# Decay rows issued by SyncE instead of ScalarE, weight loads spread out, and a new issue order, in a gated linear attention with a soft mixture of experts

## The chip, the cores and the metric

The kernel runs on one core of a Trainium2 chip. The metric is the device time of one execution in microseconds. A profile gives the span from the first to the last instruction of one execution and that execution's own time. Engines are named as in the profile: PE (matrix engine), DVE (vector engine), ACT (scalar engine), POOL (GpSimd), SP (SyncE, which here only issues DMAs). PEld is PE's weight load; ACTq and SPq are what the instruction sequencers of ACT and SP do themselves, such as issuing a DMA.

## The reference

Two stages follow each other. The first is a linear attention with a complex gate per step, for 4 batches, 8 heads, 768 steps and head dimension 48. The second treats the 3072 rows of 384 numbers that come out as tokens of a soft mixture of 8 experts with 4 slots each.

```python
scale = np.minimum(mag, 0.999) / (mag + 1e-06)          # mag = |a|
new_re = ar * S_re - ai * S_im
new_im = ar * S_im + ai * S_re
S_re, S_im = new_re + k v^T, new_im                      # per batch and head, for each t
y[:, :, t] = q^T S_re
...
logits = x @ phi                                         # x = y, 3072 x 384; phi 384 x 32
d = softmax of logits over the tokens;  slot_input = d.T @ x
slot_out[e] = relu(slot_input[e] @ w1[e]) @ w2[e]        # 384 -> 1024 -> 384
out = (softmax of logits over the slots) @ slot_out
```

## The kernel before, in words

**Blocks.** The time axis is cut into blocks of 128 steps: 24 blocks g (6 per batch), three of which make a unit u (8 units). Within a block the recurrence is written in polar form: sums of log magnitude and of phase over the steps come from a matmul with a triangular matrix, and queries and keys are scaled by exponentials of the magnitude and by sine and cosine of the phase. A state of 96x384 numbers carries from block to block within a batch.

**The stages and their names.** The whole front part is written as Python generators, one per piece of work, cut into steps at each `yield`. A string `ORDER` (L296) names, step by step, which generator runs next (`run`, L790); `_InOrder.pin` (L341) ties each engine to that order. A name that stands n times in the table runs n steps. Only the order within each engine counts; two neighbours in the table on different engines are free of each other. The names:

- `g` (gates, L603): for one unit, logarithms and exponentials of the gate, alternating DVE (L609, L615, L617, L621, L625) and ACT (L611, L613, L619, L623). The first unit is done in two parts (128x384 and 128x768), the others at once (128x1152). `t` is the arctangent (ACT L632). `L` and `T` load ACT's tables (L552 for exponential and logarithm, L555 for sine and arctangent).
- `p` (phase, L634): per block, a correction of one row from the block before (DVE L640), the matmul (PE L643, tile `up`), rounding (DVE L646, L648, tile `f`), sine and cosine (ACT L653, DVE L656, ACT L658, tile `cs`).
- `e` (expo, L663): per block the matmul (PE L667), two exponentials into the tile `ee` (ACT L671, L673), and then two small DMAs (L679) that copy the last step's row, 1x8x48, from `ee` to the tile `rrow`: the **decay rows**. There are 48 of them, and before the change ACT issues them.
- `d` (decay, L681): turns the three rows of a unit into columns `rt` (PE L684, DVE L686).
- `m` (mults, L690): multiplies `ee` in place by query and key (POOL L694; for block 0, DVE L699) and makes the tiles `hat` (DVE L703, twice a block). Because POOL overwrites `ee`, it must wait until the decay rows have been read out of it.
- `x` (transposes of `hat`, PE L715, copied by ACT L718 to `hT`), `c` (scores, PE L723, masked by DVE L727), `a` (output, PE L748 and L750, copied by ACT L753), `D` (state, PE L761, DVE L766 and L768), `f` (turns the output back, PE L773, ACT L776).
- `l`, `s` (router logits and running softmax sums), `me`, `er`, `si` (merging them, token weights, slot inputs).
- `la`, `lq`, `lv`: loads of the next unit's gates (1152 KB), queries and keys (1152 KB) and values (576 KB) into two buffers each, so that a load waits until the unit two before is done with its buffer. `w`: loads of expert weights: the first seven go to tiles of their own (`wx`, 1024 KB each), later ones into the buffers of `aat` and `qkt` and into freed memory. `wu` are matmuls without use. SP issues all of these loads in the order of the table.

After the table's end the experts run: hidden layer (PE L230), second layer (PE L250), mixing (PE L283), output DMAs (L289, L292). That part is the same code before and after.

Of the kernel before, what the change touches and what calls it, by code (L numbers as in the profile page):

```python
# [293 lines left out]


ORDER = """  # L296
    L0 lq0 w0 la0 w1 w2 w3 w4 w5 lv0 w6 g0 g0 wu1 g0 g0 wu2 g0 wu0 g0 wu3 g0 g1 g0 g0 g1 e0 g1 e0 g1 e0 e0 m0 T0 g1 t0 t1 p0 p0
    m0 p0 p0 p1 p0 L1 p1 m0 p1 x2 g1 x0 g1 p2 g1 p2 x0 g1 x2 p2 e1 g2 e2 la1 m0 g2 m0 g2 x1 x3 e1 g2 D0 e1 e1 D0 x1 x3 g2 c0 e2
    e2 c1 T1 c0 m1 c1 a0 e2 p1 a0 t2 p1 p1 p3 p2 p2 p3 m1 p2 L2 m1 x6 x4 p3 m2 x5 x4 x7 x6 d0 x5 d0 D0 x7 lq1 c2 p4 g2 c3 a0 g2
    p4 D1 c2 g2 D1 c3 a1 D1 g2 a1 D1 e3 m2 a1 e3 m2 x8 e3 x10 x8 p4 x9 x10 e3 x9 p5 e4 g3 e5 e4 e4 x11 m3 p5 x11 e4 D2 g3 p5 la2  # L300
    D2 g3 f0 D2 c4 m4 e5 e5 c5 c4 e5 T2 a2 c5 p3 p3 g3 a2 p3 p4 lv1 p4 d1 g3 f1 p4 a2 l0 p5 p5 m5 p5 l0 L3 d1 l0 l0 lq2 s0 s0 m3
    s0 g3 m3 f0 f1 g3 x13 x12 x14 s0 g3 x15 D3 x12 D3 g3 x14 x13 D2 x15 e6 m4 c6 e6 m4 e6 c7 e6 c6 x17 c7 x18 x17 D3 x16 m6 g4
    a3 x16 x18 a3 g4 D3 m5 e7 g4 x19 m5 e8 x19 g4 D4 a3 e7 D4 e7 e7 c8 g4 e8 e8 e8 c9 T3 c8 x22 c9 m7 t3 x21 D4 x20 x20 p6 x22
    m8 a4 x21 p6 a4 p6 p7 lq3 t4 p6 p7 D4 p6 x23 p7 c10 x23 c11 p8 p7 a4 p7 c10 p8 p7 c11 a5 la3 p8 a5 p9 m6 lv2 a5 m6 p8 x24
    x26 x24 p8 x25 m7 x26 x27 p8 l1 m7 L4 p9 l1 x25 D5 p9 x27 D5 g4 d2 c12 g4 c13 x29 d2 p10 g4 x28 p10 x28 g4 x29 c12 e9 p10
    x30 a6 x30 D5 e9 e10 p11 e9 c13 e9 e10 m8 e10 a6 e10 p11 m8 a6 e11 p11 m9 x31 la4 f2 x31 g5 D6 f2 D6 m10 g5 s0 f3 s0 g5 c14
    s0 f3 c15 c14 e11 e11 x32 c15 e11 T4 x33 D6 x34 D6 a7 x32 g5 x34 a7 p9 x33 p9 g5 p9 x35 D7 x35 m9 D7 t5 l1 m9 a7 p12 p10 p10
    l1 f4 m11 p10 f5 f4 p12 d3 f5 c16 d3 D7 p12 lq4 c17 p11 p11 c16 p11 x36 c17 L5 x37 p13 x38 a8 m10 s1 x36 s1 m10 s1 x38 a8
    x37 s1 D7 lv3 s1 a8 g5 p13 s1 l2 g5 x39 D8 x39 l2 s1 g5 D8 p13 c18 c19 c18 x40 c19 x42 x40 g5 x41 x42 x43 x41 x43 m11 e12
    e13 m11 e12 e12 a9 D8 e12 e13 D8 e13 a9 e13 p14 g6 p14 m12 a9 e14 p14 g6 D9 la5 D9 m13 g6 l2 l2 c20 s2 x44 s2 c20 c21 x44 D9  # L310
    e14 x46 c21 a10 x46 D9 e14 g6 T5 s2 a10 g6 e14 x45 x47 x45 s2 f6 x47 p12 f7 p12 m14 d4 f8 f6 d4 f7 c22 a10 t6 c23 c22 lq5
    p13 p13 a11 c23 p13 p15 f8 a11 m12 p14 p14 lv4 s2 m12 p14 x48 L6 s2 x50 s2 x49 m13 p15 x48 x50 x51 m13 x49 D10 x51 p15 D10
    a11 g6 l3 c24 g6 c25 l3 g6 c24 x54 x52 c25 x53 x52 g6 a12 x54 a12 D10 e15 a12 m14 x55 e15 e16 m14 e15 e15 x53 e17 p16 x55 g7
    D11 e16 e16 D11 e16 m15 p16 g7 D11 c26 g7 c27 c26 m16 e17 x58 e17 c27 x57 T6 a13 g7 e17 p15 a13 p15 g7 p15 x56 a13 l3 D12
    x56 l3 m17 x58 D12 t7 p16 x59 f9 p16 p16 lq6 d5 p16 d5 p17 f9 m15 x57 p17 x59 p18 m15 la6 f10 p18 f11 f10 f12 f11 p17 c28
    p18 f12 c29 p17 p17 c28 p17 x62 p19 L7 x61 c29 x60 D11 p19 s3 x63 x60 s3 D12 s3 x62 a14 s3 x61 D12 x63 m16 a14 m16 lv5 D13
    a14 p19 g7 D13 s3 g7 l4 c30 s3 g7 l4 s3 x64 c31 g7 x64 x66 c30 e18 x66 c31 x65 D13 e19 x65 m17 x67 a15 m17 x67 e18 D13 e18
    a15 e18 p20 p18 g8 p20 a15 e19 D14 e19 m18 p20 D14 e19 g8 e20 D14 g8 l4 l4 c32 w7 m19 c33 s4 e20 s4 c32 x69 e20 c33 T7 s4
    x68 s4 x70 g8 p18 a16 x69 x68 g8 a16 x70 e20 p19 x71 p19 m18 f13 p19 f14 x71 m18 c34 f13 f14 m20 a16 x72 c34 c35 x72 p20 x74
    p20 w8 s4 x74 p20 x73 s4 x75 L8 s4 d6 D15 d6 c35 x73 D15 D14 x75 a17 D15 g8 a17 g8 lv6 f15 m19 f16 g8 c36 m19 f15 c37 a17 g8  # L320
    f16 x77 x78 x77 c36 e21 c37 x76 a18 x76 m20 a18 x78 m20 D16 a18 e21 D16 e21 e21 e22 D16 e23 D16 e22 e22 x79 l5 x79 m21 e22
    e23 D17 l5 e23 T8 D17 l5 l5 f17 m22 e23 f18 t8 c38 f17 c39 f18 c38 m23 x80 c39 x82 x80 x81 x82 a19 x81 p21 a19 p21 a19 D17
    x83 p21 d7 x83 f19 c40 d7 p22 p21 f19 p21 c41 p21 c40 a20 c41 m21 a20 m21 x86 a20 D17 x85 x84 p22 x84 x87 x86 p22 l6 p22 p22
    D18 l6 p22 p23 D18 x85 m22 x87 p23 m22 l6 c42 w9 c43 c42 x90 c43 x88 l6 x89 x88 x91 x90 D18 a21 x89 p23 x91 a21 D18 p23 p23
    p23 D19 L9 m23 D19 c44 m23 w12 s5 x92 s6 s5 c44 s5 c45 a21 s5 x92 s6 D19 s6 s5 a22 s5 s6 s5 x94 c45 x93 x94 D19 a22 x93 x95
    c46 x95 a22 c47 c46 a23 c47 a23 f20 f21 f20 s6 a23 f21 l7 s6 f22 l7 s6 f23 f22 l7 l7 s7 me0 f23 w11 w10 er0 s7 me0 s7 er0
    er2 s7 er0 s7 er2 er7 er2 er1 er7 er7 s7 er8 ze0 er1 me0 er3 me0 s7 me0 er8 er6 me0 me0 er8 er6 me0 er3 er1 si0 er4 si0 er3
    er5 er6 er5 er4 er4 er5
"""


# [344 lines left out]
            rrow[u] = eo.tile([UB, H, 2, D], F32, name="rrow", bufs=1)  # L676
        r = LAST[par]
        for c in range(2):
            ACT.dma_start(out=rrow[u][j : j + 1, :, c, :], in_=e[r : r + 1, 0].rearrange("p (h d) -> p h d", d=D))  # L679
# [346 lines left out]
```

## Time and profile before

| what | value |
|---|---|
| three runs, median (lowest to highest) | 361.63 us (355.16 to 362.6) |
| the profiled execution | 356.5 us, span 354.7 us |
| mean granted PE clock | 0.906 of full |
| DMA moved | 54.85 MB, mean 155 GB/s |
| first stretch, 0 to 40 us | loads at 282 to 421 GB/s, PE short of work |
| middle, 40 to about 300 us | attention blocks, PE busy most of the time |
| end, from 308 us | experts and output |

A group line of the profile reads: source line, engine, operation, tiles (written <- read), count, then busy time, mean duration in ns, and the idle time of the engine just before these instructions with what ended most of it. A timeline line reads: start, duration, engine, line, operation, tiles, shapes, count, and in brackets the idle time before and what ended it. The chain that ended last is followed back from the last instruction: at each step to what released it. A line of the table by stretches has the stretch, its length, busy time of each engine with its count, the granted PE clock, the DMA engines' share, and GB/s.

### The profile page before, as it was taken

What the parts mean: (1) busy time and instruction counts of PE and PEld (TensorE: products, weight loads), DVE (VectorE), ACT (ScalarE), POOL (GpSimd) and SP (SyncE); (2) the same over time, 40 slices, a digit from 0 to 9 for tenths busy, and PEclk for the clock granted to TensorE, in tenths of its full rate; (3) what the DMA queues carried; (4) which work ended last, traced back from release to release, by engine and by line L of the source; (5) the groups of instructions that cost most, each with busy time, mean ns of one, the idle gap of its engine ahead of it and who ended that gap; (6) DMA issues with size and microseconds to landing.
All of it is one profiled execution on the core that took longest, in us unless ns stands there. A gap on an engine that the chain in (4) does not pass through costs nothing.

```text
span 354.7 us, 6884 instructions
## 1 busy us (share of the span) xinstructions
PE 301.5 (85%) x2758; PEld 229.2 (65%) x2758; DVE 244.9 (69%) x461; ACT 211.0 (59%) x373; POOL 46.6 (13%) x30
## 2 busy tenths in 40 slices
...
GB/s 264 421 420 419 246 81 71 258 9 1 135 188 13 136 111 23 69 20 140 178 2 1 266 71 1 122 118 68 3 0 2 120 354 409 145 284 421 200 290 105
DMA packets 15287, 54.85 MB, mean 155 GB/s; under 512 B 1936, under 2 KB 8976, under 8 KB 10640
## 3 DMA queue, kind: packets, MB, share of 16 engines
...
q10 hardware_dynamic: 768, 0.08, 0.2%
...
## 4 chain that ended last, share of the span: by engine, by line
PE 54%; DVE 20%; ACT 12%; issue 4%; DMA 4%; ACTq 3%; SPq 1%; DVEq 0%
PE sp L723 10%; PE tp L715 8%; PE up L643 5%; PE db L761 4%; PE hp L230 4%; PE yb L748 3%; PE op L250 3%; ACTq L679 3%; DVE scT L727 3%; DVE hat L703 3%; PE xp L773 3%; PE yb L750 3%; PE o L283 3%; PE lg L103 2%; DVE n L656 2%
## 5 line engine op out<-in xcount | busy, mean ns | idle before, releaser
L718 ACT COPY hT<-tp 96x512 f32<-96x512 f32 x96 | 51.7, 582 | 35.4 <-PE tp L715 31.9
L694 POOL TENSOR_TENSOR ee<-ee,qkt 128x768 f32<-128x768 f32 x23 | 43.8, 1905 | 216.0 <-DMA rrow<-ee 130.9
L715 PE MATMUL tp<-cst,hat 128*96 128x128 f32 x384 | 58.3, 298 | 11.2 <-DVE hat L703 7.6
L715 PEld LDWEIGHTS tp<-cst,hat 128*96 128x96 f32 x384 | 47.2, 138 | 24.6 <-issue 12.7
L723 PE MATMUL sp<-hT,hT 96*128 96x128 f32 x384 | 51.3, 287 | 1.8 <-ACT xs L776 1.0
L723 PEld LDWEIGHTS sp<-hT,hT 96*128 96x128 f32 x384 | 48.0, 201 | 3.5 <-ACT xs L776 1.2
L703 DVE TENSOR_TENSOR hat<-ee,cs 128x768 f32<-128x768 f32 x48 | 47.2, 1018 | 2.8 <-issue 1.4
L727 DVE TENSOR_TENSOR scT<-sp,cst 128x512 f32<-128x512 f32 x48 | 32.4, 686 | 15.3 <-PE sp L723 15.3
L643 PE MATMUL up<-aat,cst 128*128 128x384 f32 x48 | 24.8, 605 | 17.1 <-ACT aat L632 9.1
L748 PE MATMUL yb<-scT,vt 128*48 128x128 f32 x384 | 37.5, 282 | 1.3 <-DVE scT L727 1.0
L750 PE MATMUL yb<-hT,st 96*48 96x128 f32 x320 | 32.0, 278 | 0.0
L761 PEld LDWEIGHTS db<-vt,hat 128*96 128x96 f32 x320 | 29.7, 166 | 3.0 <-issue 1.9
L761 PE MATMUL db<-vt,hat 128*96 128x48 f32 x320 | 30.2, 248 | 0.0
L748 PEld LDWEIGHTS yb<-scT,vt 128*48 128x48 f32 x384 | 21.1, 124 | 8.2 <-issue 3.4
L643 PEld LDWEIGHTS up<-aat,cst 128*128 128x128 f32 x48 | 8.3, 215 | 22.6 <-ACT aat L632 10.2
L667 PE MATMUL lp<-aat,cst 128*128 128x384 f32 x48 | 21.4, 545 | 1.8 <-DVE aat L625 1.3
L646 DVE TENSOR_SCALAR n<-up 128x384 f32<-128x384 f32 x24 | 13.2, 550 | 13.9 <-PE up L643 13.9
L753 ACT COPY yT<-yb 128x512 f32<-128x512 f32 x24 | 14.0, 583 | 13.2 <-PE yb L750 10.9
L750 PEld LDWEIGHTS yb<-hT,st 96*48 96x48 f32 x320 | 19.7, 126 | 0.0
L658 ACT ACTIVATE cs<-n,kb 128x384 f32<-128x384 f32 x24 | 14.7, 611 | 6.7 <-DVE n L656 6.6
L623 ACT ACTIVATE gt<-aat,kb 128x1152 f32<-128x1152 f32 (+2 forms) x9 | 10.4, 1150 | 10.5 <-DVE aat L621 10.5
L671 ACT ACTIVATE ee<-lp 128x384 f32<-128x384 f32 x24 | 11.7, 488 | 7.7 <-issue 3.1
...
## 6 DMA issues: line engine op xcount, KB each, us to landing
qkt<-in_qk_dram SPq DMA_DIRECT2D x7, 1152.0 KB
aat<-in_aa_dram SPq DMA_DIRECT2D x7, 1152.0 KB
...
wx<-in_w_dram SPq DMA_DIRECT2D x5, 1152.0 KB
...
we<-in_w_dram SPq DMA_DIRECT2D x2, 1152.0 KB
wt<-in_w_dram SPq DMA_DIRECT2D x2, 1152.0 KB
```

The lines of the kernel that those rows point to most:

```text
L643: PE.matmul(out=up, lhsT=tri_u[par], rhs=ph, start=True, stop=True)
L658: ACT.activation(out=t[:, :, 0, :], in_=a.rearrange("p (h d) -> p h d", d=D), func=AF.Sin, scale=-TWO_PI, bias=kb[:, 2:3])
L667: PE.matmul(out=lp, lhsT=tri_l[par], rhs=aat[u][:, 0, j], start=True, stop=True)
L694: POOL.tensor_tensor(out=e, in0=e, in1=qkt[u][:, j], op=ALU.mult)
L703: DVE.tensor_tensor(out=x, in0=e[:, w].rearrange("p (h d) -> p h d", d=D).unsqueeze(2).broadcast_to([P, H, 2, D]), in1=cs[g], op=ALU.mult,)
L715: PE.transpose(out=tp[:, a, :], in_=hat[g][w][:, 4 * hh + a].rearrange("p c d -> p (c d)"), identity=ident)
L718: ACT.copy(out=hT[g, hh, w], in_=tp)
L723: PE.matmul(out=sp[:, a, :], lhsT=hT[g, hh, 1][:, a, :], rhs=hT[g, hh, 0][:, a, :], start=True, stop=True)
L727: DVE.tensor_tensor(out=t, in0=sp, in1=mask[g % 2].unsqueeze(1).broadcast_to([P, 4, P]), op=ALU.mult)
L748: PE.matmul(out=o, lhsT=vt[u][:, j, h, :], rhs=scT[g, hh][:, a, :], start=True, stop=first)
L750: PE.matmul(out=o, lhsT=st[g - 1][:, h, :], rhs=hT[g, hh, 0][:, a, :], start=False, stop=True)
L761: PE.matmul(out=db[:, h, :], lhsT=hat[g][1][:, h].rearrange("p c d -> p (c d)"), rhs=vt[u][:, j, h, :], start=True, stop=True)
```

## The change

Two edits. The decay rows are issued by SP instead of ACT:

```diff
         for c in range(2):
-            ACT.dma_start(out=rrow[u][j : j + 1, :, c, :], in_=e[r : r + 1, 0].rearrange("p (h d) -> p h d", d=D))
+            SP.dma_start(out=rrow[u][j : j + 1, :, c, :], in_=e[r : r + 1, 0].rearrange("p (h d) -> p h d", d=D))
```

And the table `ORDER` is another one with the same 1083 names. Its first line and its last ones show the kind of difference:

```diff
-    L0 lq0 w0 la0 w1 w2 w3 w4 w5 lv0 w6 g0 g0 wu1 g0 g0 wu2 g0 wu0 g0 wu3 g0 g1 g0 g0 g1 e0 g1 e0 g1 e0 e0 m0 T0 g1 t0 t1 p0 p0
+    g0 la0 wu1 L0 wu0 g0 g0 g0 g0 g0 g0 g0 wu3 g1 g1 g1 g1 e0 e0 e0 e0 T0 wu2 t0 p0 g1 g1 t1 p0 p0 p0 p0 lq0 L1 m0 m0 m0 x0 m0
...
-    s0 g3 m3 f0 f1 g3 x13 x12 x14 s0 g3 x15 D3 x12 D3 g3 x14 x13 D2 x15 e6 m4 c6 e6 m4 e6 c7 e6 c6 x17 c7 x18 x17 D3 x16 m6 g4
+    x14 x12 x12 x13 x13 x15 x15 p7 L3 g4 g4 g4 p7 m4 m4 m5 lv0 D3 c6 c6 D2 c7 x18 e6 e6 e6 e6 e7 e7 g4 x16 x16 e8 e7 e7 x17 x17
...
-    er5 er6 er5 er4 er4 er5
+    er5 er6 er5 er6 w10
```

The instructions are the same ones; each engine runs them in another order. Three places matter below.

**ACT at the start**, where the exponentials of block 0 end and the phase begins. Before:

```order
L671 ACTIVATE ee<-lp 128x384
L673 ACTIVATE ee<-lp 128x384
L679 DMA rrow<-ee 1x8x48 x2
L555 ACT_TABLE_LOAD
L632 ACTIVATE aat<-aat 128x384
L632 ACTIVATE aat<-aat 128x768
```

Now:

```order
L671 ACTIVATE ee<-lp 128x384
L673 ACTIVATE ee<-lp 128x384
L555 ACT_TABLE_LOAD
L632 ACTIVATE aat<-aat 128x384
L632 ACTIVATE aat<-aat 128x768
L653 ACTIVATE cs<-f 128x8x48
```

The two row DMAs are gone from ACT's queue, here and after each of the other 23 pairs of exponentials.

**SP**, after the ten loads of the first unit and the constants, which stay. Before:

```order
L567 DMA qkt<-in_qk_dram 128x2304
L596 DMA wx<-in_w_dram 128x2048
L563 DMA aat<-in_aa_dram 128x2304
L596 DMA wx<-in_w_dram 128x2048 x5
L571 DMA vt<-in_vv_dram 128x1152
L596 DMA wx<-in_w_dram 128x2048
L563 DMA aat<-in_aa_dram 128x2304
L567 DMA qkt<-in_qk_dram 128x2304
```

Now:

```order
L563 DMA aat<-in_aa_dram 128x2304
L679 DMA rrow<-ee 1x8x48 x2
L567 DMA qkt<-in_qk_dram 128x2304
L679 DMA rrow<-ee 1x8x48 x4
L563 DMA aat<-in_aa_dram 128x2304
L567 DMA qkt<-in_qk_dram 128x2304
L679 DMA rrow<-ee 1x8x48 x4
L596 DMA wx<-in_w_dram 128x2048
L679 DMA rrow<-ee 1x8x48 x2
L563 DMA aat<-in_aa_dram 128x2304
L571 DMA vt<-in_vv_dram 128x1152
L679 DMA rrow<-ee 1x8x48 x6
```

The rows stand between the loads and share SP's queue with them. Of the seven `wx` loads, one stands here, four more stand among the rows of units 3 to 6, and the last two stand behind the last row.

**DVE at the start**, from the rounded phase of block 0 on; `ee` and `hat_184` belong to block 0, 128x768 are the gates of the rest of unit 0, 128x1152 those of unit 1. Before:

```order
L703 TENSOR_TENSOR hat_184<-ee,cs 128x768
L646 TENSOR_SCALAR n<-up 128x384
L648 TENSOR_TENSOR f<-up,n 128x384
L621 SCALAR_TENSOR_TENSOR aat<-aat,gt 128x768
L640 SCALAR_TENSOR_TENSOR aat<-f,aat 1x384
L625 SCALAR_TENSOR_TENSOR aat<-aat,gt 128x768
L646 TENSOR_SCALAR n<-up 128x384
L648 TENSOR_TENSOR f<-up,n 128x384
L609 TENSOR_SCALAR gt,amin<-aat 128x1152
L699 TENSOR_TENSOR ee<-ee,qkt 128x384
L703 TENSOR_TENSOR hat_225<-ee,cs 128x768
```

Now, where the block's two `hat` tiles have the numbers 165 and 184:

```order
L703 TENSOR_TENSOR hat_165<-ee,cs 128x768
L699 TENSOR_TENSOR ee<-ee,qkt 128x384
L640 SCALAR_TENSOR_TENSOR aat<-f,aat 1x384
L621 SCALAR_TENSOR_TENSOR aat<-aat,gt 128x768
L703 TENSOR_TENSOR hat_184<-ee,cs 128x768
L625 SCALAR_TENSOR_TENSOR aat<-aat,gt 128x768
L609 TENSOR_SCALAR gt,amin<-aat 128x1152
L646 TENSOR_SCALAR n<-up 128x384
L648 TENSOR_TENSOR f<-up,n 128x384
```

The second `hat` of block 0 and the gates of unit 1 (L609) now stand ahead of the second block's phase, where they stood behind the third's.

More of the change, by code (lines that the diff above doesn't have):

```diff
@@ L305 @@
[L305 to L316, printed above, removed]
@@ L321 @@
[L321 to L324, printed above, removed]
@@ new lines @@
+    p1 p1 x2 g1 g1 g1 m0 x0 x3 x3 x1 g1 D0 g2 g2 e2 p1 p2 D0 g2 g2 g2 e2 e2 e2 m2 e1 e1 e1 e1 x1 x2 p2 g2 T1 p1 p1 c0 p2 c0 c1
+    d0 d0 D0 p1 a0 c1 t2 p2 a0 a0 p2 p2 la1 L2 m1 m1 x6 x6 m1 x4 D1 x4 g2 g2 D1 m2 f0 f0 x8 x8 x5 x5 p3 m2 p3 x7 x7 x9 x11 x11
+    g2 D1 e3 e3 e3 g3 p3 g3 D1 g3 c3 c3 c2 e4 x9 e4 e4 e5 e5 D2 c2 a1 g3 p4 lq1 e5 e5 x10 e4 m4 g3 g3 p4 w0 a1 a1 p4 p5 x10 g3
+    g3 c4 c4 p5 D2 p5 T2 c5 c5 a2 a2 t3 p6 p3 a2 g3 p3 D2 p3 p6 p5 p5 e3 m3 p4 p4 p5 f2 m3 m3 p7 p4 l0 l0 f2 la2 f1 f1 d1 d1 x14
@@ new lines @@
+    x14 x12 x12 x13 x13 x15 x15 p7 L3 g4 g4 g4 p7 m4 m4 m5 lv0 D3 c6 c6 D2 c7 x18 e6 e6 e6 e6 e7 e7 g4 x16 x16 e8 e7 e7 x17 x17
+    D3 x18 a3 c7 a3 g4 g4 a3 m5 x22 m5 x22 m6 p8 x19 e8 x19 e8 e8 g4 p8 D3 p8 g4 f3 g4 D3 x21 la3 f3 x20 c8 x21 c8 D4 T3 c9 c9
+    l0 D4 d2 t4 D4 x23 l0 p6 lq2 g5 a4 a4 d2 x20 c10 x23 c11 p7 p7 p6 p7 p9 p8 p9 a4 p6 D4 c10 p8 p8 a5 c11 a5 m6 x24 x26 p9 p10
+    m6 m7 L4 s0 a5 m7 m7 s0 s0 p10 p10 x27 x24 g5 g5 x27 x26 s0 lv1 D5 D5 D5 x25 x31 x31 m8 x25 x30 x30 x28 x28 e9 e9 e9 e9 c13
```

36 lines of the change are left out of this document (23 added, 13 removed).

## The prediction

> **What bounds the kernel now.** I read the page's busy times first, then the chain that ended last, then the stretches, then the timeline at the start and at one unit's border.
>
> ```profile
> PE 301.5 (85%) x2758; PEld 229.2 (65%) x2758; DVE 244.9 (69%) x461; ACT 211.0 (59%) x373; POOL 46.6 (13%) x30
> PE 54%; DVE 20%; ACT 12%; issue 4%; DMA 4%; ACTq 3%; SPq 1%; DVEq 0%
> by line: PE sp L723 9.7%; PE tp L715 8.1%; PE up L643 4.7%; PE db L761 4.4%; issue 4.0%; PE hp L230 3.5%; PE yb L748 3.4%; PE op L250 3.1%; ACTq L679 3.0%; DVE scT L727 2.9%; DVE hat L703 2.7%; PE xp L773 2.6%; PE yb L750 2.6%; PE o L283 2.
> L679 ACTq DMA_DIRECT2D rrow<-ee x48: 621/622/1232, 12.3 to 256.6; - x48
> ```
>
> PE is the busiest engine but holds only 54% of the chain; the chain jumps between engines, so each in-order queue matters. ACT computes for 211.0 us; the 48 row issues at 622 ns (median) add 48 x 0.622 = 29.9 us to its sequencer, and 3.0% of the 354.7 us span, 10.6 us, of them lie on the chain.
>
> ```profile
> 0.00:10.00 10.00, 4.63 (x8) 2.06 (x8) 3.65 (x11) 3.56 (x5) 0.20 (x4) 1.00 0.79 282
> 10.00:20.00 10.00, 3.08 (x6) 0.80 (x4) 4.70 (x11) 5.74 (x9) 0.00 (x0) 0.76 1.02 421
> 20.00:30.00 10.00, 7.80 (x16) 3.58 (x16) 8.33 (x13) 5.74 (x8) 0.00 (x0) 0.56 1.01 419
> 30.00:40.00 10.00, 6.55 (x58) 5.21 (x58) 6.92 (x10) 7.45 (x12) 2.29 (x2) 1.00 0.89 355
> 60.00:80.00 20.00, 15.16 (x145) 13.22 (x144) 15.93 (x27) 15.01 (x26) 3.94 (x2) 0.83 0.43 148
> 120.00:140.00 20.00, 17.73 (x144) 15.42 (x143) 14.53 (x28) 15.53 (x28) 4.68 (x3) 0.78 0.34 119
> 220.00:240.00 20.00, 16.43 (x128) 13.01 (x128) 13.02 (x23) 14.11 (x27) 5.46 (x3) 0.84 0.29 107
> 260.00:280.00 20.00, 19.74 (x223) 17.10 (x225) 14.26 (x29) 9.85 (x19) 0.20 (x1) 1.00 0.16 54
> 310.00:320.00 10.00, 10.00 (x84) 2.71 (x76) 0.42 (x1) 0.60 (x1) 0.00 (x0) 0.89 0.74 288
> ```
>
> Three regimes. To 40 us PE (first busy column) is short of work and the DMA engines are full. In the middle PE has 0.3 to 4.8 us idle in 20, and where it idles, the granted clock drops too (0.78 to 0.84). From 310 us PE is full and the code is unchanged.
>
> **The start.** ACT and PE up to the first sines, then where blocks 0 and 1 get their `hat`:
>
> ```profile
> 12.32 1.89 ACTq L679 DMA_DIRECT2D rrow<-ee  x2
> 14.24 1.28 ACT L555 ACT_TABLE_LOAD   x1 [1.57 <-issue]
> 15.53 1.26 ACT L632 ACTIVATE aat<-aat 128x384 f32<-128x384 f32 x2
> 16.11 1.65 PE L643 MATMUL up<-aat,cst 128*128 128x384 f32 x2 [4.51 <-ACT aat L632]
> 18.91 0.56 DVE L699 TENSOR_TENSOR ee<-ee,qkt 128x384 f32<-128x384 f32 x1
> 20.42 0.96 DVE L703 TENSOR_TENSOR hat<-ee,cs 128x768 f32<-128x768 f32 x1
> 27.34 1.34 DVE L609 TENSOR_SCALAR_CACHE_REDUCE gt<-aat 128x1152 f32<-128x1152 f32 x1
> 37.71 3.96 POOL L694 TENSOR_TENSOR ee<-ee,qkt 128x768 f32<-128x768 f32 x2 [37.25 <-ACT aat L632]
> 38.17 0.91 PE L643 MATMUL up<-aat,cst 128*128 128x384 f32 x2 [1.25 <-DVE aat L640]
> 39.93 3.42 DVE L703 TENSOR_TENSOR hat<-ee,cs 128x768 f32<-128x768 f32 x2
> 12.67 0.88 ACTq L679
> 13.58 5.20 DMA rrow<-ee
> 31.85 0.26 ACTq L679
> 32.15 0.62 ACTq L679
> 34.66 0.26 ACTq L679
> ```
>
> The last five rows are of the chain: a row issued at 13.58 landed 5.20 us later, while the loads ran at 421 GB/s. Now the table load follows the exponentials directly. The bracket is the gain: 1.57 us earlier for the table, the arctangent, `up` and the first sine. In the new DVE order unit 1's gates (27.34) stand ahead of the second phase instead of behind the third. By the rows above and the DVE work before them I put L609 about 2.2 to 3.5 us earlier: first `hat` at 20.42 - 1.6 = 18.8, ended 19.8; L640, L699 and L621 end near 21.8; second `hat` 1 us, L625 1 us, then L609 at 23.8 instead of 27.34. Against this, the second block's rounding comes behind L609, so its wrap and the third `up` are some 2 us later than before. The next common point is the `hat` of block 1, at 39.93, which followed POOL's first multiply (37.71 + about 2). POOL needs the rows of blocks 1 and 2; their exponentials follow unit 1's gates on ACT and come some 3 us earlier, and their rows land faster, since the seven weight loads no longer run then. Earliest case 6 us, latest 2 us (the two issues and nothing else). I take **-4.0 us**, nearer the middle, since both parts have a row.
>
> **The middle.** One unit's border:
>
> ```profile
> 86.62 1.28 ACTq L679 DMA_DIRECT2D rrow<-ee  x2
> 88.02 0.49 ACT L671 ACTIVATE ee<-lp 128x384 f32<-128x384 f32 x1 [1.06 <-PE sp L723]
> 88.54 1.27 ACTq L679 DMA_DIRECT2D rrow<-ee  x2
> 89.84 1.28 ACT L555 ACT_TABLE_LOAD   x1 [0.95 <-ACT ee L673]
> 91.14 1.16 ACT L632 ACTIVATE aat<-aat 128x1152 f32<-128x1152 f32 x1
> ```
>
> ACT's datapath stands idle 1.06 and 0.95 us while its sequencer issues rows, though the page names other releasers; behind it wait table, arctangent and the next `up`. So a pair of issues costs ACT about 1 us, not 1.25: the rest overlaps the exponential before it. Of the 10.6 us on the chain 2.0 (0.88 + 0.26 + 0.62 + 0.26) lie at the start, which is counted; 8.6 are left. If PE's own queue is next behind each (nothing won) the term is 0; if ACT alone was late, -8.6. PE with 54% and DVE with 20% of the chain are close behind, so I take half: **-4.3 us**.
>
> The clock: one minus the clock times 20 us is 3.4, 4.4 and 3.2 us of PE time lost in the three dipping stretches, 11.0 together. Shorter waits at the borders should save a little of it. Bounds: +3 (one more dip) to -8; I take **-2.0 us**, because the clock is low in the stretches where PE waits, and ACT's queue is one of several things it waits for there.
>
> **Rows on SP's queue.** The 29.9 us of issue move to SP, which computes nothing; its time is hidden as long as loads are not late. The cost is the row's way.
>
> ```profile
> 55.44 1.31 ACTq L679 DMA_DIRECT2D rrow<-ee  x2
> 57.97 1.81 POOL L694 TENSOR_TENSOR ee<-ee,qkt 128x768 f32<-128x768 f32 x1 [16.30 <-DMA rrow<-ee]
> 70.94 1.81 DVE L703 TENSOR_TENSOR hat<-ee,cs 128x768 f32<-128x768 f32 x2
> aat<-in_aa_dram SPq DMA_DIRECT2D x7, 1152.0 KB
> SPq L567 <- POOL ee L694: 73.1, 6, 25.8
> L703 DVE TENSOR_TENSOR hat<-ee,cs 128x768 f32<-128x768 f32 x48 | 47.2, 1018 | 2.8 <-issue 1.4 <-PE tp L715 1.0
> ```
>
> With quiet DMA engines a pair issued from 55.44 let POOL start at 57.97. POOL ends at 59.78, and the `hat` that reads it starts at 70.94: 11.2 us of slack; over the kernel DVE's `hat` waited 2.8 us, none of it mainly on POOL. A load of 1152 KB at 421 GB/s takes 2.8 us, so a row behind one is 2.8 us late, behind two 5.6. SP also holds a row while a load ahead waits for its buffer (73.1 us in six waits of L567). In the new order such a load waits for a multiply or a phase of an earlier unit, which POOL and PE run before that row's own multiply anyway. Each row also makes SP wait for ACT's exponential; queued behind it are the loads of a later unit, for which that unit's gates (DVE L609) and multiplies (POOL) wait, and their turn comes a unit later. I count **0**; bounds 0 and +19.6 (a load on each of seven units, nothing hidden).
>
> [...]
>
> **Weights.** Seven `wx` loads of 1024 KB leave the first 40 us; five run in the middle, where the DMA share is 0.16 to 0.43, two behind the last row. Covered by PE's work up to 310 us: 0. With that cover gone, two loads: 2 x 1024 KB at 421 GB/s, +5.0 us.
>
> **Sum.** 356.5 - 4.0 - 4.3 - 2.0 + 0 + 0 = 346.2, say **346 us**. The sum stands against the profiled execution (span 354.7, own time 356.5); the median of the three runs is 361.63, 1.4% above, so a median of the new kernel may lie as far above my figure.
>
> **Rivals.**
> 1. *PE hides it.* The issues on the chain are replaced by PE work of equal length, the clock does not move: 356.5 - 4.0 = 352.5. For: PE 19.74 of 20 us in 260 to 280. Against: 4.8, 2.3 and 3.6 us of idle in the three dipping stretches.
> 2. *Rows stuck behind loads.* The place is POOL's multiply ahead of `hat`, which DVE runs in order, so everything behind waits. It decides from the point where the new order leaves less time between a block's exponential and its `hat` than row, load and multiply take; then 2.8 us for each of seven units: 356.5 - 4.0 - 4.3 + 19.6 = 367.8. For: the 5.20 us row, SP's long waits. Against: 11.2 us of slack.
> 3. *The clock stays up.* PE's idle of 4.51 us before the first `up` shrinks to about 2.3 (1.57 earlier, and one spare matmul now between), and the clock, 0.76 and 0.56 from 10 to 30 us, stays full. `up` then takes 0.91 instead of 1.65 us; three of them make 2.2 us, and one whole dip of the middle saved makes 4.4: 346.2 - 2.2 - 4.4 = 339.6. [...]
>
> **How the numbers follow.** My sum 0.40, rival 1 0.27, rival 2 0.17, rival 3 0.16. Two per cent of 356.5 is 7.1 us, about what a measurement of this kernel can tell from no change: under 349.4 is faster, over 363.6 slower. The sum's own range, from the bounds of its terms, is 339 to 353; six sevenths of it is faster: 0.34, with rival 3 0.16 and a little of rival 1, 0.53. Slower: rival 2 and a bad order, 0.18. The rest, 0.29, is within. The range runs from 334, below rival 3, to 364, short of rival 2 in full.
>
> **What would show it.** Right: ACT's table load at about 12.7 us with no 1.57 us idle; block 1's `hat` near 36; no ACTq L679 on the chain; POOL's waits on rows still long but `hat` not waiting for POOL; the stretches 60:80, 120:140 and 220:240 at a higher clock. Wrong: DVE `hat` idle with POOL as releaser, rows landing over 5 us after issue in the middle (rival 2); PE's 4.8, 2.3 and 3.6 us of idle as before with no ACTq left on the chain (rival 1); hidden-layer matmuls waiting for weights.

## The result and the profile after

The changed kernel takes 318.06 us (median of four runs, 316.07 to 319.39), the kernel before 360.57 us in the same comparison (four runs). The ratio is 0.8896 with a 95% interval of 0.8761 to 0.9031: 11% faster, and 16 us below the lower end of the predicted range. Ratios here leave disturbed runs out, so they can differ by a per cent from the quotient of two medians.

The profiled execution took 316.07 us with a span of 314.2 us; before, 356.5 and 354.7. The busy times and the chain that ended last:

```profile
PE 280.0 (89%) x2758; PEld 220.8 (70%) x2758; DVE 242.4 (77%) x461; ACT 207.8 (66%) x373; POOL 54.1 (17%) x30
PE 53%; DVE 32%; ACT 7%; DMA 3%; issue 2%; SPq 0%; ACTq 0%; DVEq 0%
L703 DVE TENSOR_TENSOR hat<-ee,cs 128x768 f32<-128x768 f32 x48 | 47.5, 1018 | 0.6 <-ACT cs L658 0.4
```

PE runs the same 2758 instructions in 280.0 us instead of 301.5. So of the 40.5 us that the span lost, 21.5 are not fewer waits but a faster PE, and the other 19.0 are less idle time of PE (span minus busy: 53.2 before, 34.2 now). The mean granted clock says the same: one minus the clock times the span is 33.3 us of PE time lost before (0.906) and 11.9 us now (0.962). Of the 21.5 us, 19.1 lie between ACT's third load of the exponential table (40.7 us before, 35.3 now) and the first hidden-layer matmul (308.0 and 268.7), almost none before that, and 2.3 in the experts, whose code is the same. ACT's queue is gone from the chain, and `hat` waits for 0.6 us instead of 2.8.

The stretches that the prediction showed:

```profile
10.00:20.00 10.00, 4.68 (x12) 2.28 (x12) 6.19 (x11) 7.83 (x11) 0.00 (x0) 0.87 0.83 322
20.00:30.00 10.00, 9.24 (x50) 6.86 (x49) 8.91 (x14) 7.59 (x12) 0.63 (x1) 0.79 0.01 1
30.00:40.00 10.00, 8.08 (x61) 7.23 (x61) 9.65 (x13) 9.19 (x13) 2.96 (x2) 0.73 0.67 238
60.00:80.00 20.00, 18.45 (x172) 15.97 (x171) 19.84 (x28) 18.68 (x30) 8.90 (x4) 1.00 0.15 52
120.00:140.00 20.00, 20.00 (x198) 17.10 (x197) 17.50 (x30) 14.19 (x25) 7.78 (x4) 1.00 0.39 143
220.00:240.00 20.00, 19.92 (x233) 18.29 (x233) 13.07 (x26) 12.72 (x25) 1.49 (x1) 1.00 0.62 257
```

The three dips of the middle (0.83, 0.78, 0.84) are gone; the clock is full from 41 to 304 us. The DMA engines rest from 20 to 30 us, since the weights come later. At the start:

```profile
11.97 1.55 SPq L679 DMA_DIRECT2D rrow<-ee  x2
12.34 1.28 ACT L555 ACT_TABLE_LOAD   x1
14.21 0.91 PE L643 MATMUL up<-aat,cst 128*128 128x384 f32 x2 [1.93 <-ACT aat L632]
22.60 1.35 DVE L609 TENSOR_SCALAR_CACHE_REDUCE gt<-aat 128x1152 f32<-128x1152 f32 x1
29.37 3.59 POOL L694 TENSOR_TENSOR ee<-ee,qkt 128x768 f32<-128x768 f32 x2 [28.91 <-DMA rrow<-ee]
33.10 1.81 DVE L703 TENSOR_TENSOR hat<-ee,cs 128x768 f32<-128x768 f32 x2
```

The table load follows the exponentials with no bracket, `up` takes 0.91 instead of 1.65 us, and block 1's `hat` starts at 33.10 instead of 39.93.

### The profile page after: what moved, and what is told of

Same layout as the page of the kernel before. It is cut to its first block, busy times and chain, and to the rows that moved or that the text cites. A ratio compares the mean times of both kernels' runs of the same rounds, so it can differ in the third digit from the quotient of the medians.

```text
span 314.2 us, 6918 instructions
## 1 busy us (share of the span) xinstructions
PE 280.0 (89%) x2758; PEld 220.8 (70%) x2758; DVE 242.4 (77%) x461; ACT 207.8 (66%) x373; POOL 54.1 (17%) x30
## 4 chain that ended last, share of the span: by engine, by line
PE 53%; DVE 32%; ACT 7%; DMA 3%; issue 2%; SPq 0%; ACTq 0%; DVEq 0%
PE tp L715 9%; PE sp L723 7%; DVE hat L703 7%; PE db L761 5%; PE yb L748 4%; PE op L250 4%; PE hp L230 3%; DVE scT L727 3%; PE yb L750 3%; DVE aat L621 3%; PE up L643 3%; PE o L283 3%; PE xp L773 2%; DVE f L648 2%; DVE n L646 2%
## 5 line engine op out<-in xcount | busy, mean ns | idle before, releaser
L694 POOL TENSOR_TENSOR ee<-ee,qkt 128x768 f32<-128x768 f32 x23 | 51.4, 2246 | 169.6 <-DMA rrow<-ee 123.1
L715 PE MATMUL tp<-cst,hat 128*96 128x128 f32 x384 | 56.3, 285 | 8.8 <-DVE hat L703 8.7
L715 PEld LDWEIGHTS tp<-cst,hat 128*96 128x96 f32 x384 | 44.2, 132 | 18.1 <-issue 13.3
L761 PEld LDWEIGHTS db<-vt,hat 128*96 128x96 f32 x320 | 32.3, 173 | 2.3 <-issue 1.1
L761 PE MATMUL db<-vt,hat 128*96 128x48 f32 x320 | 32.6, 252 | 0.1
L748 PEld LDWEIGHTS yb<-scT,vt 128*48 128x48 f32 x384 | 21.1, 122 | 12.0 <-DVE scT L727 6.8
L643 PE MATMUL up<-aat,cst 128*128 128x384 f32 x48 | 21.6, 533 | 3.5 <-ACT aat L632 2.4
L667 PE MATMUL lp<-aat,cst 128*128 128x384 f32 x48 | 19.5, 498 | 0.0
L646 DVE TENSOR_SCALAR n<-up 128x384 f32<-128x384 f32 x24 | 13.2, 550 | 5.5 <-PE up L643 5.4
L776 ACT COPY xs<-xp 128x384 f32<-128x384 f32 x24 | 11.1, 476 | 8.5 <-PE xp L773 8.4
L285 ACT ACTIVATE os<-o,rc 128x256 f32<-128x256 f32 (+1 forms) x24 | 9.7, 420 | 9.7 <-PE o L283 7.1
L287 DVE TENSOR_SCALAR os<-o,rc 128x256 f32<-128x256 f32 (+1 forms) x24 | 9.8, 417 | 8.1 <-PE o L283 5.9
```

The source lines that it names most:

```text
L643: PE.matmul(out=up, lhsT=tri_u[par], rhs=ph, start=True, stop=True)
L646: DVE.tensor_scalar(out=n, in0=up, scalar1=MAGIC, scalar2=MAGIC, op0=ALU.add, op1=ALU.subtract)
L667: PE.matmul(out=lp, lhsT=tri_l[par], rhs=aat[u][:, 0, j], start=True, stop=True)
L694: POOL.tensor_tensor(out=e, in0=e, in1=qkt[u][:, j], op=ALU.mult)
L715: PE.transpose(out=tp[:, a, :], in_=hat[g][w][:, 4 * hh + a].rearrange("p c d -> p (c d)"), identity=ident)
L748: PE.matmul(out=o, lhsT=vt[u][:, j, h, :], rhs=scT[g, hh][:, a, :], start=True, stop=first)
```

## The experiments

Theory at this point: two of the change's parts are worth more than the prediction gave them, because each wait of PE that goes also spares a stretch at half clock, and the new order itself shortens the middle, which the sum had not counted. Rival: one part (the rows off ACT) does it all, and order and weights only ride along. The early or spread weights, which belong to the new table, are taken as a part of their own. All kernels compute the full result; some add useless work, which is said there. "Idle" is span minus PE busy, "clock" is span times one minus the mean granted clock, both of the profiled execution; half clock during a wait counts in both, so the two must not be added. Diffs of the table show pieces of its lines.

| run | order | rows issued by | weights | median us | ratio, 95% interval | span | idle | clock |
|---|---|---|---|---|---|---|---|---|
| before | old | ACT | early | 360.57 | 1 | 354.7 | 53.2 | 33.3 |
| D | old | ACT | spread | 349.88 | 0.987, 0.978 to 0.996 | 347.9 | 50.7 | 26.4 |
| E | old | SP | early | 360.43 | 1.021, 1.007 to 1.034 | 360.3 | 65.8 | 34.6 |
| C | old | SP | spread | 339.17 | 0.958, 0.948 to 0.967 | 336.3 | 44.4 | 22.5 |
| B | new | ACT, late | early | 343.46 | 0.970, 0.959 to 0.981 | 341.4 | 51.7 | 26.6 |
| A | new | ACT, late | spread | 347.45 | 0.978, 0.968 to 0.989 | 346.4 | 51.3 | 31.9 |
| G | new | ACT | spread | 331.26 | 0.941, 0.928 to 0.954 | 329.2 | 42.0 | 21.7 |
| F | new | SP | early | 338.73 | 0.961, 0.942 to 0.980 | 335.9 | 57.1 | 21.8 |
| the change | new | SP | spread | 318.06 | 0.890, 0.876 to 0.903 | 314.2 | 34.2 | 11.9 |

The kernel before had medians from 355.25 to 360.57 us in the six comparisons.

### The three parts, each alone and together (A to G)

A, B and G are the new order with the rows on ACT. In A and B they stand where the new table has them; in G directly behind the block's exponentials:

```diff
-            SP.dma_start(out=rrow[u][j : j + 1, :, c, :], in_=e[r : r + 1, 0].rearrange("p (h d) -> p h d", d=D))
+            ACT.dma_start(out=rrow[u][j : j + 1, :, c, :], in_=e[r : r + 1, 0].rearrange("p (h d) -> p h d", d=D))
```

B and F load the weights early again, and with them the first loads of unit 1 (the first line of the new table reads `g1 g1 g1 g0` ahead of its first `e0`, not four times `g1` as printed in the section on the change):

```diff
-    g0 la0 wu1 L0 wu0 g0 g0 g0 g0 g0 g0 g0 wu3 g1
+    lq0 w0 la0 w1 w2 w3 w4 w5 lv0 w6 g0 wu1 L0 wu0 g0 g0 g0 g0 g0 g0 g0 wu3 g1
```

C and D are the old order with the seven weight loads spread (C with the rows on SP too), E the old order with only the rows on SP:

```diff
-    L0 lq0 w0 la0 w1 w2 w3 w4 w5 lv0 w6 g0 g0 wu1
+    L0 lq0 la0 lv0 g0 g0 wu1
...
-    la2 D2 g3 f0 D2 c4
+    la2 w0 D2 g3 f0 D2 c4
```

The expectations:

> The new order and the spread weights, with the decay rows issued by ACT again. If the order of the stages brought the gain (theory ORDER), most of the 42 us stays: 318 to 328 us, PE clock still near 1.00 from 60 to 300 us. If the freed ACT queue brought it (theory ROWS), the time goes back by the 17 us of ACT idle or more, with its clock dips: 340 to 358 us. If the quiet DMA engines brought it (theory LOADS), nothing changes: 316 to 320 us.

> The new order of all compute stages, but rows on ACT and the seven weight loads at the start as before: only the order of the stages is new. ORDER: 320 to 332 us, the start a few us later than in the change. ROWS or LOADS: back near before, 345 to 360 us.

> The old order of the stages, with both DMA edits: rows on SP, weights spread. ORDER: the ACT queue's freed time gives what the prediction gave it, 4 to 10 us, so 347 to 356 us. ROWS: most of the gain, 318 to 335 us.

> The old order of the stages with rows on ACT; only the seven weight loads move from the start to places behind later units' loads. ORDER or ROWS: within 4 us of before (355 to 361 us), the rows of block 0 landing in about 2 us instead of 5. LOADS: 335 us or less.

> The new order and the spread weights, rows on ACT, but each pair of rows directly behind its two exponentials in ACT's queue, not at the late place that the new table gives SP. In the run with the rows at that late place PE stood idle 7.4 us for one row that ACT issued behind two gate operations. If that lateness was most of the 29 us between that run and the change (theory LATE ROWS), this gives 322 to 332 us. If the 48 issues themselves cost the time in a queue that the new order fills (theory ISSUE TIME), it stays at 338 to 350 us.

> The kernel before with the rows on SP and nothing else: the first rows now stand behind seven weight loads of 1024 KB in SP's queue. Rows stuck behind loads: block 0's first multiply (DVE L699) waits until some 30 us instead of 18.9, time 350 to 362 us, 10 us or more over the run with spread weights and rows on SP. If rows pass loads, 336 to 342 us as in that run.

> The change with the seven weight loads, and the first loads of unit 1, at the start as before. Rows stuck behind loads: the start is late by 10 to 15 us, time 328 to 335 us. If rows pass loads: 316 to 322 us.

What was measured, by the table. A lies in the range of ROWS, G in that of LATE ROWS, E in that of rows stuck behind loads; B, C and D lie between the ranges of their theories, and F 4 us above its higher one. No part brings the gain alone. From before to the change one part at a time: weights spread, about -5 us (D's ratio of 0.987; 7 by the medians, 357.15 to 349.88); rows to SP, -10.7 (D to C); new order, -21.1 (C to the change). Undone from the change's side, the rows are worth 13.2 us (G), the weights 20.7 us (F). So the parts are not independent. With rows on ACT the spread weights are worth some 5 us in the old order, and in the new one with its late rows they even cost 4 (B 343.46, A 347.45, with intervals that overlap). With rows on SP they are worth 21 us in either order (E to C 21.3, F to the change 20.7), because without the spreading the first rows stand behind the loads. The queue of SP and the chain in F:

```profile
9.55 5.10 SPq L596 DMA_DIRECT2D wx<-in_w_dram  x5
22.14 28.48 SPq L679 DMA_DIRECT2D rrow<-ee  x6
```

```profile
9.55 15.00 DMA wx<-in_w_dram
24.57 13.41 DMA rrow<-ee
38.10 0.57 DVE ee L699
```

SP, still issuing loads, reaches the first rows only at 22.14. The second of them, issued at 24.57, lands 13.41 us later, at 37.98, and the first DVE multiply of `ee` follows at once. PE waits 23.6 us there in one piece, 3.39 in the change. E has the same row (13.43 us) and a wait of PE of 23.2 us. That is rival 2 of the prediction, real and of its size, but at one place and hidden by the third part of the change. Before the change, on ACT's queue beside the same loads, this row landed 5.20 us after its issue (13.58).

A against G shows that the place of the issue in ACT's order matters as much as the issue. In A it stands behind the gates, and PE idles 7.39 us. A's chain there:

```profile
130.90 1.07 ACT aat L611
131.99 0.67 ACT gt L613
132.69 2.52 DMA rrow<-ee
135.37 1.81 POOL ee L694
137.21 0.97 DVE hat L703
138.22 1.09 PE tp L715 x4
```

So A and B price the new order too low; G (331.26) is the fair one, 18.6 us below D.

### Where in the kernel the order's 21 us lie (I, J, M to P)

The first guess was one mechanism: in the old table the arctangents of units 2, 4 and 7 come in the same period of ACT's sine table as the unit's first phase, right ahead of it; in the new table all come a period earlier. I moves two of them ahead in the old order (base C), J moves six back in the new one, each with the first phase steps behind it:

```diff
-    p4 a2 l0 p5 p5 m5 p5 l0 L3 d1 l0
+    p4 a2 l0 p5 p5 m5 p5 l0 t3 L3 d1 l0
```

```diff
-    p5 T2 c5 c5 a2 a2 t3 p6 p3 a2 g3 p3
+    p5 T2 c5 c5 a2 a2 p3 a2 g3 p3
...
-    T3 c9 c9 l0 D4 d2
+    T3 t3 p6 p6 p7 p7 p7 p8 p8 p8 c9 c9 l0 D4 d2
```

> The table of before with the rows on SP and the weights spread (339.17 us, ratio 0.9575), and in it the arctangents of units 2 and 7 moved one trigonometric period of ACT ahead, with the gate steps of their unit that they need. The order is then the old one in all else. Theory 'arctangent a period ahead' (the new table is faster because a unit's gates and arctangent are done a whole period before its first phase, so that PE does not stand before the first up): PE's waits of over 2 us before the up of these two units go, and the time is 4 to 8 us below 339, 331 to 335 us (ratio 0.934 to 0.946). Rival 'no single place' (the gain of the new table is spread over many small waits, the arctangent was not what PE waited for once the rows were off ACT): 337 to 341 us, and the gaps stay or come up elsewhere.

> The changed kernel, with the arctangents of units 2 to 7 moved one period of ACT later, behind the table load of the unit's own first phase, and the first phase steps that stood ahead of it moved behind them. Nothing else is changed. Theory 'arctangent a period ahead': PE stands before the first up of these units for 1.3 to 2.5 us each, as it did in the kernel before (2.34, 2.27 and 2.98 us at three places), and the clock drops behind some of them: 8 to 15 us above 318, 326 to 333 us (ratio 0.914 to 0.934). Rival 'no single place': 316 to 322 us (ratio 0.885 to 0.903), since up has other work of PE ahead of it.

I: 344.62 us, ratio 0.972 (0.964 to 0.981), 5 us slower than C. J: 384.82 us, ratio 1.086 (1.074 to 1.098), 67 us slower than the change, over four times the most that was expected. J's largest group of PE's waits (sum, count, longest) and one of its units:

```profile
PE up L643 <- DVE aat L640: 29.4, 13, 5.5
```

```profile
125.05 1.16 ACT L632 ACTIVATE aat<-aat 128x1152 f32<-128x1152 f32 x1
126.25 0.55 DVE L640 SCALAR_TENSOR_TENSOR aat<-f,aat 1x384 f32<-1x384 f32 x1 [2.81 <-ACT aat L632]
126.85 1.43 PE L643 MATMUL up<-aat,cst 128*128 128x384 f32 x2 [4.14 <-DVE aat L640]
130.10 1.65 PE L643 MATMUL up<-aat,cst 128*128 128x384 f32 x2 [1.82 <-DVE aat L640]
```

J lays the chain arctangent, `up`, rounding, row correction, next `up` bare three times a unit: about 3.3 us from one `up` to the next, on PE. It shows what a late arctangent costs when nothing stands between the three phases. It doesn't show that the old order pays this: there other work stands between them, and I won nothing, since with the rows off ACT (C) PE no longer waited at those two places. The guess falls.

The second approach splices the two orders (rows on SP, weights spread): one table up to an ACT table load, then what is left in the other order. The cuts are the third and the fifth load of the exponential table, at 35.3 and 87.5 us in the change.

```diff
     a0 c1 t2 p2 a0 a0 p2 p2 la1
-    L2 m1 m1 x6 x6 m1 x4 D1 x4
+    lv0 m1 p3 p3 m1 L2 m1 x6 x4 p3 x5 x4 x7 x6
```

(The change and M around the first cut; O has the same at the second, N and P the counterparts.)

> Rows on SP and weights spread, as in the change. The new table up to ACT's third load of the exponential table (35.3 us in the changed kernel, 41.7 in the kernel that has the old table), then what is left in the old order. Between the old table throughout (339.17 us, ratio 0.9575) and the change (318.06, 0.8896) lie 21 us. Theory 'start': they come from the first 80 us, where the change has 8.2 of its 10.2 us less idle of PE; this kernel wins at least the 6.4 us of the earlier load: 326 to 333 us (ratio 0.92 to 0.94). Theory 'later': they come from the order behind it, and the early lead is lost again at the next common wait: 336 to 340 us.

> The counterpart: the old table up to the same load, then what is left in the new order. Theory 'start': 324 to 332 us, as the 6.4 us of the start are missing. Theory 'later': 316 to 321 us (ratio 0.885 to 0.90). If this one and its counterpart together win much less or much more than 21 us, the parts depend on each other.

> As the first of these, with the cut at ACT's fifth load of the exponential table (87.5 us in the change, 101.2 with the old table). Theory 'start': nearly the whole gain is there, 318 to 324 us (ratio 0.89 to 0.91). Theory 'later': the gain comes in equal parts along the middle, so about a third of it is missing and the 13.7 us at the cut are what stays, 325 to 331 us (ratio 0.91 to 0.93), or less if it is lost again.

> The counterpart of the third: the old table up to ACT's fifth load of the exponential table, then the new one. Theory 'start': 334 to 339 us (ratio 0.94 to 0.957), nothing left to win. Theory 'later': 328 to 333 us, the 7 us behind the cut are won.

| run | median us | ratio, 95% interval |
|---|---|---|
| M: new to the first cut, then old | 338.40 | 0.952, 0.945 to 0.960 |
| O: new to the second cut, then old | 330.90 | 0.928, 0.918 to 0.938 |
| N: old to the first cut, then new | 326.86 | 0.912, 0.902 to 0.922 |
| P: old to the second cut, then new | 342.08 | 0.959, 0.950 to 0.968 |

The profiles by stretches, cut at the two loads and at the first hidden-layer matmul; C and then the change:

```profile
8.00:41.70 33.70, 21.98 (x83) 14.18 (x82) 20.38 (x33) 20.57 (x30) 3.59 (x2) 0.75 0.50 193
41.70:101.20 59.50, 51.96 (x487) 43.29 (x487) 48.43 (x80) 43.74 (x73) 10.88 (x6) 0.91 0.38 142
101.20:289.80 188.60, 180.67 (x1788) 148.34 (x1780) 152.41 (x294) 131.34 (x239) 33.87 (x18) 0.98 0.37 140
```

```profile
8.00:35.30 27.30, 19.31 (x97) 12.43 (x96) 22.20 (x36) 21.80 (x32) 3.59 (x2) 0.86 0.56 205
35.30:87.50 52.20, 49.02 (x444) 40.73 (x444) 48.76 (x76) 42.66 (x68) 16.58 (x6) 0.94 0.33 128
87.50:268.70 181.20, 173.85 (x1811) 147.38 (x1808) 152.90 (x295) 128.68 (x243) 33.74 (x18) 1.00 0.42 160
```

The new order wins 6.4, 7.3 and 7.4 us in the three parts. In the profiles the spliced kernels carry each part's length with them (M 27.8, 59.7, 190.7; O 27.8, 55.1, 190.2; N 34.4, 54.1, 185.6). In the times they do so only in part: M wins 0.8 and O 8.3 us over C, N loses 8.8 us to the change, and P 24.0, so that P is no better than C. (The profiled executions of N and P were the longest of their four.) Put in from the front, the three parts are worth 0.8, 7.5 and 12.8 us (C, M, O, the change); put in from the end, the last one costs 2.9, the one between the cuts wins 15.2 and the start 8.8 (C, P, N, the change). The ratios' intervals reach some 2.5 to 3.7 us to each side. So neither "start" nor "later" holds alone (M fits "later", N "start", O "later", P neither): the part between the cuts weighs most on the mean of the two ways, and the new order's last part pays only behind its own middle part; why, the runs don't settle.

For the start and for the part between the cuts the traces show a cause, and both times it is the landing of a row. SP's queue at the start of C, and the chain:

```profile
6.51 0.70 SPq L567 DMA_DIRECT2D qkt<-in_qk_dram  x1
7.25 0.43 SPq L563 DMA_DIRECT2D aat<-in_aa_dram  x1
8.75 0.33 SPq L571 DMA_DIRECT2D vt<-in_vv_dram  x1
13.34 1.55 SPq L679 DMA_DIRECT2D rrow<-ee  x2
14.20 6.05 DMA rrow<-ee
```

All three loads of unit 1 stand ahead of the first rows. The second row lands 6.05 us after its issue, DVE waits 2.71 us for it at its first multiply of `ee` (20.37; 16.62 in the change), and behind that the second `up` comes after 5.35 us of idle PE. In the change only the gates' load stands ahead of these rows, neither DVE nor the second `up` waits, and that is the new order's doing. G, which has the new order too, has ACT's two issues (0.88 and 0.63 us) on its chain ahead of the table load instead. I, N and P, which have the old order at the start, wait as C does (6.4, 6.0 and 6.2 us before the second `up`); M and O, which have the new one, don't. So the start's 6.4 us need both edits.

For the part between the cuts, C's queue of SP and chain:

```profile
56.33 0.43 SPq L563 DMA_DIRECT2D aat<-in_aa_dram  x1
56.81 1.25 SPq L596 DMA_DIRECT2D wx<-in_w_dram  x1
58.79 1.34 SPq L679 DMA_DIRECT2D rrow<-ee  x2
64.78 0.51 PE L684 MATMUL rp<-cst,rrow 3*96 3x3 f32 x8 [3.04 <-DMA rrow<-ee]
```

```profile
58.79 5.71 DMA rrow<-ee
```

A row issued behind two large loads lands 5.71 us later, PE waits 3.04 us, and 10.2 us at half clock follow (65.8 to 76.0). M, I and P, which have the old order there, show the same wait (2.8, 3.2 and 4.0 us); the change, N and O, which have the new one, don't have it. It is not the shared queue that makes it: D has the same order and loads, and its rows on ACT's own queue:

```profile
57.12 1.65 SPq L596 DMA_DIRECT2D wx<-in_w_dram  x1
59.49 1.28 ACTq L679 DMA_DIRECT2D rrow<-ee  x2
65.56 0.51 PE L684 MATMUL rp<-cst,rrow 3*96 3x3 f32 x8 [3.39 <-DMA rrow<-ee]
```

D's row lands 5.52 us after its issue (59.49), and PE waits 3.39 us. SP's queue in the change, at the same units:

```profile
48.56 2.70 SPq L679 DMA_DIRECT2D rrow<-ee  x4
51.31 0.44 SPq L596 DMA_DIRECT2D wx<-in_w_dram  x1
51.80 1.33 SPq L679 DMA_DIRECT2D rrow<-ee  x2
53.23 0.39 SPq L563 DMA_DIRECT2D aat<-in_aa_dram  x1
```

The gates' load comes behind the rows here, so that no row stands behind two loads, and PE comes to these rows (L684) only at 59.97, 8.2 us after the issue at 51.80, without a wait for them.

### What a wait of PE costs through the clock (H, K, L, Q, R)

H fills PE's waits in the kernel before with 11 useless matmuls; Q fills the two waits that the change has left at its start with four. K and R make PE stand idle at three places of the change's middle (a matmul reads a tile, POOL sets it to zero 36 or 12 times, a second matmul reads it); L puts four useless matmuls at each of the same places.

```diff
+    def stand(x):
...
+        PE.matmul(out=wp[:, 0:8], lhsT=ident, rhs=hold[:, 0:8], start=True, stop=True)
+        for _ in range(36):
+            POOL.memset(hold, 0.0)
...
+        PE.matmul(out=wp[:, 0:8], lhsT=ident, rhs=hold[:, 0:8], start=True, stop=True)
...
-    x58 lv4 x58 c26 c26
+    x58 lv4 x58 wi0 c26 c26
```

> The kernel before with 11 matmuls without use added on PE, just ahead of the instructions for which PE idled (two before the first router logits, one before the transposes of block 3, two each before the first phases of units 2 and 4, one before the phase of block 17, three before the transposes of block 18): about 11 us of PE work in gaps of about 13 us. If idle gaps bring the granted clock down and the lost clock is a large part of the gap to the change (theory CLOCK): the half-clock stretches near 70, 94, 131, 199 and 233 us go, PE busy without the added work falls by 8 us or more, time 342 to 352 us. If the clock is no matter of these gaps: 357 to 368 us, the added work at best hidden.

> The changed kernel, with PE made to stand idle at three places in the stretch from 100 to 170 us: a matmul reads a tile, POOL sets this tile 36 times to zero, and a second matmul reads it again, so PE waits some 4 us for POOL each time. To be read beside its control with useless matmuls of about the same length at the same places. Theory 'a wait of PE costs more than its length, through the clock' (each wait of over some 2 to 3 us in the trace of before was followed by a stretch of 3.4 to 10 us at half clock): half-clock stretches appear behind the three places, and the time is 12 us of waits plus 2 to 5 us of slower PE for each: 336 to 345 us. Rival 'the clock only follows the waits, it costs nothing of its own': 328 to 331 us, as much as the control with matmuls.

> The control: the changed kernel with four useless matmuls of about 1 us at each of the same three places, so that PE is held for some 4 us three times but is never idle. Both theories: PE is on the path in the middle, so the 12 us come out in full or nearly, no half-clock stretch appears, and the time is 326 to 331 us (ratio 0.914 to 0.928). If it comes out under 322, PE had slack at these places, and the runs say little of the clock's price.

> The changed kernel with four more useless matmuls in PE's two waits of the start (one in the 1.93 us before the first up, three in the 3.39 us before the first transposes). Theory 'clock': the two half-clock stretches of the start (6.8 us each from 17.4 and 34.5 us, 3.8 us of lost PE time up to the second load of the exponential table) shorten or go, and 1 to 4 us are won: 314 to 317 us (ratio 0.88 to 0.887). Rival: at the start PE waits for ACT and DVE anyway and the matmuls win nothing, 317 to 320 us; if they run late into the transposes, up to 2 us are lost.

> As the kernel in which PE stands idle at three places, with 12 writes of POOL instead of 36, so that PE waits about 3 us each time instead of 6.7 to 8.3 us. Those long waits were each followed by 10.2 us at half clock and cost 25 us in all; three stretches of useless matmuls at the same places cost 3 us. Theory 'a wait of 3 us is enough': half-clock stretches of 3.4 us or more follow, and the time is 5 to 12 us above the change, 323 to 330 us (ratio 0.903 to 0.925). Rival 'only longer waits': no half-clock stretch in the middle, 318 to 323 us.

| run | median us | ratio, 95% interval | span | PE busy | idle | clock |
|---|---|---|---|---|---|---|
| H | 351.56 | 0.992, 0.985 to 0.999 | 352.4 | 304.4 | 48.0 | 21.8 |
| K: three waits of 8.0, 8.3, 6.7 us | 343.29 | 0.967, 0.960 to 0.975 | 341.9 | 290.4 | 51.5 | 31.8 |
| R: three waits of 3.9, 4.2, 2.3 us | 333.19 | 0.939, 0.933 to 0.944 | 326.1 | 286.9 | 39.2 | 18.3 |
| L: useless matmuls there | 321.41 | 0.906, 0.902 to 0.910 | 319.0 | 288.3 | 30.7 | 11.8 |
| Q: start filled | 317.99 | 0.894, 0.889 to 0.899 | 312.2 | 279.2 | 33.0 | 6.6 |

K's three stretches behind its waits, and R's:

```profile
165.50:175.70 10.20, 4.14 (x20) 3.28 (x23) 1.60 (x2) 0.58 (x1) 7.67 (x36) 0.50 0.44 169
199.70:209.90 10.20, 4.63 (x18) 3.93 (x19) 0.89 (x1) 0.58 (x1) 5.56 (x32) 0.50 0.00 0
240.60:250.80 10.20, 6.16 (x36) 5.87 (x39) 2.00 (x6) 1.87 (x4) 8.25 (x25) 0.50 1.01 423
```

```profile
163.10:169.90 6.80, 6.80 (x52) 5.00 (x54) 4.59 (x5) 2.71 (x3) 3.41 (x2) 0.50 0.37 150
193.90:200.70 6.80, 6.80 (x31) 6.07 (x32) 1.08 (x2) 2.84 (x8) 1.61 (x1) 0.50 0.00 0
231.40:234.80 3.40, 3.40 (x20) 3.18 (x21) 2.32 (x5) 1.59 (x4) 3.40 (x3) 0.50 1.01 422
```

Each wait is followed by a stretch at exactly 0.50; L, with PE held busy at the same places, has none there and costs 3.4 us for 8.3 us of added PE work. K lies in its range of 336 to 345. By its own expectation L, being under 322, shows that PE had slack there, so K and L together say little of the clock's price. R is the cleaner measure: its waits add 10.3 us, PE busy grows by 6.9 us with nothing added to compute but twelve matmul records of 8 columns, and the span grows by 11.9. So of the span's growth more than half is the clock. In the part where the three waits stand, from ACT's fifth load of the exponential table to the hidden layer, it is 14.8 us (196.0 for 181.2), 9.4 of them PE's busy time; the parts around it came out 2.9 us shorter. The profiled execution (328.21 us) is the shortest of R's four; the others took 333 to 335 us with a mean clock of 0.918 to 0.934 instead of 0.944, so R's median lies 3 us above its range. Q is a miss for "clock": all half-clock stretches before the experts are gone (mean 0.979), the profiled span is 2.0 us shorter, and the median is the change's own. At the start PE waits for ACT and DVE whatever its clock. H ends at the upper edge of its "clock" range and won under 1%: the half-clock stretches near 94, 131 and 199 us are gone, those near 70 and 233 are not (now from 76.6 and 230.2), and the filling leaves the waits of the other engines. In these runs a price of the clock showed in the time only in the middle, where other engines wait for PE.

## Why the prediction was wrong, point by point

**What bounds the kernel: right.** PE in the middle, with its queue and ACT's and DVE's close behind it. PE still holds 53% of the chain; ACT and its queue fell from 15% to 7%, DVE rose from 20% to 32%.

**Start, -4.0: right in mechanism, too small.** The table load came at 12.34 (12.7 said), L609 at 22.60 (23.8 said), block 1's `hat` at 33.10 (36 said): 6.8 us, not 4.0, just beyond the "earliest case" of 6. The attribution was incomplete: neither the rows on SP in the old order (C, the load at 41.7) nor the new order alone (G, 41.8) brings anything by the third table load, which is at 40.7 before; only both together do (35.3). C still waits for a late row (6.05 us), G still pays ACT's issues.

**ACT rows in the middle, -4.3, bounds 0 to -8.6: mis-sized.** D to C measures -10.7, G to the change -13.2. The bound was made from the time that the issues hold on the chain. It left out that PE's waits behind them also halve the clock: from D to C the span falls by 11.6 us, of which 6.3 are idle time of PE and 5.3 its busy time.

**The clock, -2.0, bounds +3 to -8: the step that failed most.** PE busy fell by 21.5 us with the same instructions. The sentence behind the term, "ACT's queue is one of several things it waits for there", took the waits as given; but weights, rows and order each remove waits, and the larger waits bring 3.4 to 10.2 us at half clock each. I had the numbers: 11.0 us were worked out for three 20 us stretches alone, while 33.3 us of the whole span are lost at a mean clock of 0.906, 18.4 of them between the third table load and the hidden layer, where the change loses 3.0.

**The new order: not in the sum at all outside the start.** It is worth 21 us with rows on SP, of which 14.7 lie behind the start. The prediction followed the order at ACT's start, SP's and DVE's, and treated the rest, without a reason, as worth nothing. This step and the clock overlap: of the 22.1 us of span from C to the change 10.2 are idle time of PE and 11.9 its busy time.

**Rows on SP, 0: right for the change, wrong as a statement on the edit.** `hat` waits for no row, and POOL's waits on rows are as long as before (123.1 us; 130.9 before). But the 11.2 us of slack that the 0 rests on is POOL's in the middle; DVE's multiply of block 0 and PE's turning of the rows (L684) have none in the old order, where C's DVE waits 2.71 us and its PE 3.04 us for rows. In front of the early loads E and F lose 21 us. The upper bound of 19.6 us had the right size with the wrong picture: one row behind the whole queue at the start, not one load in each of seven units.

**Weights, 0: mis-sized.** About -5 us with rows on ACT in the old order and -21 with rows on SP. With rows on SP the price of their early place was not bandwidth for PE but the rows' place behind them. With rows on ACT, from before to D, PE's idle falls by 2.5 us and its busy time by 4.3 in the profiles; which wait this follows from stays open.

**Rivals.** Rival 3 pointed the right way, with 339.6 us, but named the start's clock, which did not stay full (0.87, 0.79, 0.73) and which Q shows to be worth little or nothing (2.0 us of one span, none of the median). Rival 1 is refuted by C and G, rival 2 shown by E and F and avoided in the change.

**Range and chances.** The range of 339 to 353 is narrower than the bounds of the terms added up, 333.9 to 357.5 with nothing for rows and weights, and of its 14 us not six sevenths but three quarters lie under 349.4. Neither matters for the miss: 318 us lie below every sum of the bounds.
